# Sliding-window attention and a softplus layer on one core: bias through the matrix engine for the first 512 tokens, and a new order of steps

## Chip, core, metric

The kernel runs on one core of a Trainium2 chip. The metric is the device time of one execution in microseconds; the kernel before takes 218.93 us (median of 3 runs, 218.56 to 219.73). The engines are named as in the profile: PE multiplies matrices (PEld is its load of the stationary operand), DVE works on vectors, ACT evaluates functions, POOL is used here for starting loads, SP for starting stores and transposes by DMA.

## What is computed

Attention over 4 batches of 768 tokens with 8 heads of 64, in which a token sees at most the 96 tokens up to itself and the first 8 tokens of its batch, with a bias that falls with distance; then a two-layer network with a softplus between, on all 3072 tokens.

```python
scores = scale * np.matmul(q, k.transpose(0, 1, 3, 2))
is_global = pos[None, :] < int(n_global)               # 8
is_local = (rel >= 0) & (rel < int(n_local))           # 96
dist = np.where(is_global & ~is_local, float(n_local), np.abs(rel))
bias = -slopes[:, None, None] * dist[None, :, :]       # slopes 2^-1 .. 2^-8
scores = np.where(keep, scores + bias, -1e9)
a = np.exp(scores - max);  a = a / sum;  x = a @ v     # per head, heads side by side: 512 wide
h = x @ w_in                                           # 512 -> 2048
out = softplus(h) @ w_out                              # 2048 -> 512
```

## The kernel before

**Tiling.** The tokens are cut into 24 blocks of 128 (n = 0 to 23, six to a batch) for the attention, and into 12 chunks of 256 (c = 0 to 11, two blocks each) for the network. A block's keys are its own 128 and the block before; the 8 first tokens of the batch are copied over rows of the earlier block that lie outside the window (gk for keys, gv for values). The first block of a batch has its own keys alone.

**The attention of a block**, in halves of four heads: q and k are brought to [feature, token] form, either by transposes on PE through PSUM and copies by DVE (t, blocks 2 to 7; tr_in, to_QT, to_KT), or by DMA transposes that SP starts (d, from block 8 on; dma_qk). sc multiplies keys by queries (16 or 8 matmuls of 64 rows a half, two heads side by side in the array) into the two PSUM banks s_ps; DVE adds the bias table on the way from PSUM to the tile Z in SBUF (add_bias, lines 271 and 273); ACT takes the exponential from Z to Pb (ex, line 295). pv multiplies Pb by the values, with a column of ones for the sum, into x_ps (line 308), and DVE divides (lines 319 and 322). tr_x turns the result to [feature, token] form in XT, on PE for blocks 0 to 5 and by DMA from block 6 on. From block 8 on, sc does both halves at once, the second in two other banks ("tr" and "o2").

**The network.** ffn1 (f) is one of eight steps of a chunk: eight matmuls of 256 columns into one of two banks hT, then on ACT an exponential and a logarithm (lines 358 and 359) into G. ffn2 (o) is one of eight steps: four matmuls of 512 columns into the bank "o" (or "o2"); after four of them DVE copies the bank and SP stores it. Steps are numbered through: f8 is the first of chunk 1. f0, f1 of a chunk need w_in's piece 0, f2, f3 piece 1, and so on; o0 and o4 need w_out's piece 0, o1 and o5 piece 1.

**Loads** are all on POOL's queue and change float32 to bfloat16 on the way: l loads q and k of a block, lv its v, load_w_in and load_w_out a quarter of a matrix. Only block 0's q and k come through SP, as float32 (q_f, k_f), and are cast by DVE (lines 472 and 473). q and k have 4 buffers each in turn, v has 8. In the built program each POOL transfer from the ninth on waits for the landing of the one eight before it. gate (g) holds POOL until a given f step's G is written.

**Order.** A manual schedule: each engine runs its instructions in the order in which the code issues them. `opening()` does the two blocks 0 and 1 with 28 filler matmuls on zeros (warm, 512 columns each; 8 in front, 20 between steps). Bias tables in float32 are made before that, by 24 multiplies on ACT (lines 187 and 191). Then come the steps of the string ORDER, by hand, up to f27, and from there a rule by due times: `steady(n)` for a block (s at 4n - 10.4), f at u + 0.5, o at u + 13.9.

Of the kernel before, what the change touches and what calls it, by code (L numbers as in the profile page):

```python
# [19 lines left out]
def kernel(  # L20
# [11 lines left out]
    nc = tc.nc  # L32
# [50 lines left out]
    q_f = const.tile([P, H, D], F32, name="q_f")  # L83
    k_f = const.tile([P, H, D], F32, name="k_f")
    nc.sync.dma_start(q_f[:], q[0, :, 0:P, :].rearrange("h s d -> s h d"))
    nc.sync.dma_start(k_f[:], k[0, :, 0:P, :].rearrange("h s d -> s h d"))

    def ones(lo, hi):
        for n in range(lo, hi):
# [6 lines left out]
    def load(n, src, dst):  # L96
        b, i = divmod(n, BPB)
        nc.gpsimd.dma_start(  # L98
            dst[n][:, :, 0:D], src[b, :, i * P : (i + 1) * P, :].rearrange("h s d -> s h d")
        )  # L100

    def load_w_in(c):
        nc.gpsimd.dma_start(  # L103
            w_in_c[c][:],
            moe_w_in[:, c * FW : (c + 1) * FW].rearrange("(m p) f -> p m f", p=P),
        )
# [14 lines left out]
    def load_block(n):  # L121
        load_qk(n)
        load_v(n)
# [11 lines left out]


    ident = const.tile([P, P], BF16, name="ident")
    dist_0 = const.tile([P, P], F32, name="dist_0")
    dist_d = const.tile([P, P], F32, name="dist_d")
    dist_p = const.tile([P, P], F32, name="dist_p")  # L140
    bias0 = const.tile([P, 2, 4, P], F32, name="bias0")
    biasA = const.tile([P, 2, 8, P], F32, name="biasA")

    rampf = const.tile([P, P], F32, name="rampf")
    far_a = const.tile([P, P], F32, name="far_a")
# [3 lines left out]
        allow_small_or_imprecise_dtypes=True,  # L149
    )  # L150
    make_identity(nc, ident)
    load(1, q, q_t)
    load(1, k, k_t)
    load(0, v, v_t)
    load(1, v, v_t)
    load_w_in(0)
    load_w_in(1)

    def tables():
        nc.vector.tensor_scalar(  # L160
            far_a[:], rampf[:], float(NL - 1), FAR, op0=ALU.is_gt, op1=ALU.mult
        )
        nc.vector.tensor_scalar(far_b[:], rampf[:], 0.0, FAR, op0=ALU.is_lt, op1=ALU.mult)
        nc.vector.tensor_tensor(far_a[:], far_a[:], far_b[:], ALU.add)
        nc.vector.tensor_tensor(dist_d[:], far_a[:], rampf[:], ALU.add)
        nc.vector.tensor_copy(dist_0[:], dist_d[:])
        nc.vector.tensor_scalar_min(dist_0[0:NG, :], dist_0[0:NG, :], float(NL))
        nc.vector.tensor_scalar(
            far_b[:], rampf[:], -float(P - NL + 1), FAR, op0=ALU.is_gt, op1=ALU.mult
        )  # L170
        nc.vector.scalar_tensor_tensor(dist_p[:], rampf[:], float(P), far_b[:], ALU.add, ALU.add)
        nc.vector.memset(dist_p[0:NG, :], float(NL))

    tables()
    ones(2, RV)

    load_block(2)
    load_block(3)
    load_w_in(2)
    load_w_in(3)  # L180

    def head_of(half, r):
        return 4 * half + 2 * ((r // 2) % 2) + r // 4

    def bias_first(half):
        for r in range(0, 8, 2):
            nc.scalar.mul(bias0[:, half, r // 2, :], dist_0[:], -slopes[head_of(half, r)])

    def bias_rest(half):
        for r in range(8):  # L190
            nc.scalar.mul(
                biasA[:, half, r, :], (dist_p if r % 2 else dist_d)[:], -slopes[head_of(half, r)]
            )

    s_ps = ps.tile([P, 8, P], F32, name="s_ps")
    x_ps = ps.tile([P, 4, D + 1], F32, name="x_ps")
# [7 lines left out]
    def qk_bank():  # L204
        return ps.tile([P, 2, NPAIR, P], BF16, tag="tr", name="tr")

    def tr_in(tr, j, src):
        for m in range(NPAIR):
            nc.tensor.transpose(  # L209
                tr[:, j, m, :], src[:, 2 * m : 2 * m + 2, :].rearrange("p a b -> p (a b)"), ident[:]  # L210
            )

    def to_QT(n, tr):
        QT[n] = work4.tile([P, NPAIR, P], BF16, tag="QT", name="QT")
        nc.vector.tensor_copy(QT[n][:], tr[:, 0, :, :])

    def to_KT(n, tr, copy):
        KT[n] = work4.tile(
            [P, NPAIR, P], BF16, tag="KT0" if n == first_of(n) else "KT", name="KT"
        )  # L220
        copy(KT[n][:], tr[:, 1, :, :])
# [53 lines left out]
    def sc(n, half):  # L275

        qk(n, half, lambda r: s_ps[:, r, :])
        if n < NBT:
            add_bias(n, half)
            return  # L280
        s_lo = ps.tile([P, 4, P], F32, tag="tr", name="s_lo")
        s_hi = ps.tile([P, 4, P], F32, tag="o2", name="s_hi")
        qk(n, 1, lambda r: (s_lo if r < 4 else s_hi)[:, r % 4, :])
        add_bias(n, 0)
        step, bias = (2, bias0) if n == first_of(n) else (1, biasA)
        w = 4 // step
        Z = new_Z(n, 1)
        for i, s_i in enumerate((s_lo, s_hi)):
            regs = slice(i * w, i * w + w)
            nc.vector.tensor_tensor(Z[:, regs, :], s_i[:, 0:4:step, :], bias[:, 1, regs, :], ALU.add)  # L290

    def ex(n, half):
        nreg = 4 if n == first_of(n) else 8
        Pb = work.tile([P, 8, P], BF16, tag="Pb", name="Pb")
        nc.scalar.activation(  # L295
            Pb[:, 0:nreg, :], Zt.pop((n, half))[:, 0:nreg, :], AF.Exp, scale=inv_sqrt
        )
        Pt[n, half] = Pb
# [60 lines left out]
        nc.scalar.activation(G[c][:, 2 * u : 2 * u + 2, :], e_sb[:], AF.Ln, bias=1.0)  # L359

    def o_bank(i):
        return ps.tile([P, DM], F32, tag="o2" if i else "o", name="o")

    def ffn2(c, u):
        if c == NCH - 1 and u >= NWC:
# [41 lines left out]
    def gate(s):  # L407
# [2 lines left out]
        nc.gpsimd.tensor_copy(gate_t[:], G[c][0:1, 2 * u + 1, 0:1])  # L410


    LAG = 13
    KINDS = {
        "t": tr_qk, "d": dma_qk, "gk": gk, "gv": gv, "s": sc, "e": ex, "p": pv, "x": tr_x,
        "l": load_qk, "lv": load_v, "g": gate,
# [2 lines left out]


    ORDER = """
        f0 gv2 gk2 t2 l6 lv6 f1 s2.0 e2.0 f2 t3 l7 lv7 s2.1 e2.1 gk3 f3 p2.0 s3.0 e3.0 f4 p2.1
        gv3 s3.1 e3.1 gk4 f5 x2 p3.0 f6 t4 p3.1 f7 x3 s4.0 f8 f9 e4.0 s4.1 t5 f10 g9 l8 gk5 e4.1
        f11 gv4 o4 p4.0 o0 o1 s5.0 f12 p4.1 o5 o6 e5.0 x4 gv5 s5.1 e5.1 f13 p5.0 o2 t6 o7 p5.1
        s6.0 e6.0 o3 t7 f14 g13 l9 s6.1 d8 p6.0 e6.1 f15 x5 s7.0 o8 o9 p6.1 e7.0 s7.1 gk8 f16
        g15 lv8 d9 p7.0 x6 e7.1 o10 f17 f18 g17 l10 p7.1 f19 s8.0 x7 d10 f20 g19 lv9 e8.0 gv8
        gk9 o11 e8.1 f21 f22 g21 l11 p8.0 s9.0 o12 p8.1 o13 e9.0 gv9 o14 e9.1 f23 p9.0 f24 f25
        p9.1 x8 f26 x9 gk10 gv10 o15 f27
    """

    def steady(n):

        s = 4 * n - 10.4
        return {
            f"d{n}": s - 8.2, f"gv{n}": s - 0.95, f"gk{n}": s - 0.9, f"s{n}.0": s,
            f"e{n}.0": s + 0.7, f"e{n}.1": s + 1.7, f"p{n}.0": s + 1.95, f"p{n}.1": s + 2.95,
            f"x{n}": s + 3.25,
        }

    def run(name):  # L440
        kind = name.rstrip("0123456789.")
        nums = [int(i) for i in name[len(kind):].split(".")]
        if kind in "fo":
            (ffn1 if kind == "f" else ffn2)(*divmod(nums[0], NU))
        else:
            KINDS[kind](*nums)

    warm_ps = ps2.tile([P, DM], F32, tag="hT", name="warm_ps")

    def warm(count):  # L450

        for _ in range(count):
            nc.tensor.matmul(warm_ps[:], warm_in[:, 0:P], warm_in[:])  # L453

    def tr_first_q(n):
        tr = qk_bank()
        tr_in(tr, 0, q_t[n])
        to_QT(n, tr)

    def tr_first_k(n):  # L460
        tr = ps.tile([P, 2, NPAIR, P], BF16, tag="o2", name="tr_k")
        tr_in(tr, 1, k_t[n])
        to_KT(n, tr, nc.vector.tensor_copy if n == 0 else nc.scalar.copy)

    def opening():

        warm(8)
        bias_first(0)
        bias_first(1)
        bias_rest(0)  # L470
        bias_rest(1)
        nc.vector.tensor_copy(q_t[0][:], q_f[:])
        nc.vector.tensor_copy(k_t[0][:], k_f[:])
        tr_first_q(0)
        warm(1)
        tr_first_k(0)
        warm(2)
        sc(0, 0)
        ex(0, 0)
        tr_first_q(1)  # L480
        tr_first_k(1)
        warm(1)
        sc(0, 1)
        ex(0, 1)
        warm(1)
        pv(0, 0)
        sc(1, 0)
        ex(1, 0)
        warm(1)
        pv(0, 1)  # L490
        warm(2)
        sc(1, 1)
        tr_x(0)
        ex(1, 1)
        warm(3)
        pv(1, 0)
        warm(5)
        pv(1, 1)
        warm(3)
        tr_x(1)  # L500
        warm(1)

    opening()
    load_block(4)
    load_block(5)
    for c in range(NWC):
        load_w_out(c)
    first_steps = ORDER.split()
    for name in first_steps:
        run(name)  # L510
    todo = {}
    for n in range(NBT, NB):
        todo.update(steady(n))
    for n in range(RV, NB):
        for name, u in (f"l{n}", 4 * n - 23), (f"lv{n}", 4 * n - 17):
            todo[f"g{u}"] = u + 1.6
            todo[name] = u + 1.7
    for u in range(NU * NCH):
        todo[f"f{u}"] = u + 0.5
        todo[f"o{u}"] = u + LAG + 0.9  # L520
    for name in sorted(todo.keys() - set(first_steps), key=lambda x: (todo[x], x)):
        run(name)


# [33 lines left out]
```

## Time and profile before

| What | us or share |
|---|---|
| median of 3 runs | 218.93 |
| profiled execution, span | 217.8 |
| PE busy | 209.4 (96%) |
| ACT busy | 163.2 (75%) |
| DVE busy | 116.4 (53%) |
| first f matmul starts | 16.11 |
| first f matmul with PE on the chain to the end | 30.55 |
| last store issued | 215.18 |

The costliest groups, as line, engine and operation, output<-input, shape and count, then busy us and mean ns of one, then the idle time in front of them and what ended it:

```profile
L353 PE MATMUL hT<-XT,w_in 128*128 128x256 bf16 x768 | 98.5, 273 | 0.6 <-DVE XT L340 0.3
L373 PE MATMUL o<-w_out,G 128*128 128x512 bf16 x368 | 92.4, 379 | 0.0
L358 ACT ACTIVATE e_sb<-hT 128x512 f32<-128x512 f32 x96 | 56.4, 588 | 23.5 <-PE hT L353 23.2
L295 ACT ACTIVATE Pb<-Z 128x1024 bf16<-128x1024 f32 (+1 forms) x48 | 46.7, 976 | 11.6 <-DVE Z L273 9.4
L273 DVE TENSOR_TENSOR Z<-s_ps,biasA 128x1024 f32<-128x1024 f32 x26 | 31.8, 1222 | 10.7 <-PE s_ps L259 9.2
L453 PE MATMUL warm_ps<-warm_in 128*128 128x512 bf16 x28 | 9.6, 452 | 1.2 <-DVE warm_in L93 1.2
```

A matmul's duration runs to its end, and consecutive matmuls overlap: f matmuls start 0.109 us apart though each lasts 0.273. A PE that is "busy" can therefore still stand between steps, and the distance between starts says what a step costs.

### The profile page before, as it was taken

Reading aid. Unit: us, or ns where it says so; the run is one execution under the profiler, and the core shown is the slowest. Engines: PE = TensorE matmul, PEld = TensorE weight load, DVE = VectorE, ACT = ScalarE, POOL = GpSimd, SP = SyncE. Lnnn points to the kernel's source line nnn. Section 1 sums busy time; section 2 is a strip of 40 time slices with the busy share of each in tenths; the row PEclk is TensorE's granted clock in tenths of the full one; section 3 lists DMA queues with packets and bytes.
Section 4 is the critical chain, followed back from the end, with each engine's and each line's share of the span. In section 5 each row is a group of like instructions: output and inputs, shape, how many; then the busy total and the mean of one; then the engine's idle time right before and its main releaser. Section 6 shows DMA issues by size and latency. Waiting matters only on the chain.

```text
span 217.8 us, 5046 instructions
## 1 busy us (share of the span) xinstructions
PE 209.4 (96%) x2004; PEld 142.0 (65%) x2004; DVE 116.4 (53%) x259; ACT 163.2 (75%) x266; POOL 73.9 (34%) x117
## 2 busy tenths in 40 slices
PE   7788899999999999999999999999999999999993
PEld 2347776666768767666666666666667667666553
DVE  5874965688583454464664664464574573011121
ACT  7737899467999988769779779868978978777200
POOL 8947583331434623524424324333311000000000
PEclk9999999999999999999999999999999999999998
DMA  9999999999999999999999999999992620211112
GB/s 127 162 177 187 172 193 207 164 138 149 109 112 160 150 131 189 128 127 130 143 98 155 140 106 145 145 126 117 154 138 53 98 73 9 66 51 48 48 48 96
DMA packets 110072, 27.06 MB, mean 124 GB/s; under 512 B 102625, under 2 KB 107105, under 8 KB 110049
## 3 DMA queue, kind: packets, MB, share of 16 engines
q0 software_dynamic: 77024, 13.37, 83.2%
q1 hardware_dynamic: 33024, 13.38, 33.5%
q8 instruction: 15, 0.25, 0.5%
q14 instruction: 9, 0.07, 0.1%
HBM read 27.26 MB, written 6.29 MB: 154 GB/s over the span
## 4 chain that ended last, share of the span: by engine, by line
PE 84%; DMA 6%; POOL 4%; ACT 3%; DVE 1%; issue 0%; POOLq 0%; DVEq 0%
PE o L373 37%; PE hT L353 36%; DMA k_t<-in_k_dram 5%; PE x_ps L308 4%; PE s_ps L259 3%; PE s_lo L259 1%; ACT Pb L295 1%; POOL q_t L98 1%; POOL v_t L98 1%; ACT G L359 1%; ACT e_sb L358 1%; PE tr L209 1%; POOL k_t L98 1%; PE o L395 1%; DMA out_dram<-osb 1%; POOL w_in L103 1%
## 5 line engine op out<-in xcount | busy, mean ns | idle before, releaser
L353 PE MATMUL hT<-XT,w_in 128*128 128x256 bf16 x768 | 98.5, 273 | 0.6 <-DVE XT L340 0.3
L373 PE MATMUL o<-w_out,G 128*128 128x512 bf16 x368 | 92.4, 379 | 0.0
L353 PEld LDWEIGHTS <-w_in 128*128 128x128 bf16 x768 | 74.0, 98 | 25.3 <-issue 0.7
L358 ACT ACTIVATE e_sb<-hT 128x512 f32<-128x512 f32 x96 | 56.4, 588 | 23.5 <-PE hT L353 23.2
L359 ACT ACTIVATE G<-e_sb 128x512 bf16<-128x512 f32 x96 | 60.4, 630 | 3.5
L295 ACT ACTIVATE Pb<-Z 128x1024 bf16<-128x1024 f32 (+1 forms) x48 | 46.7, 976 | 11.6 <-DVE Z L273 9.4
L373 PEld LDWEIGHTS <-G 128*128 128x128 bf16 x368 | 32.2, 97 | 27.3
L273 DVE TENSOR_TENSOR Z<-s_ps,biasA 128x1024 f32<-128x1024 f32 x26 | 31.8, 1222 | 10.7 <-PE s_ps L259 9.2
L319 DVE RECIPROCAL rcp<-x_ps 128x4 f32<-128x4 f32 x48 | 8.6, 180 | 49.0 <-PE x_ps L308 49.0
L379 DVE COPY osb<-o 128x512 f32<-128x512 f32 x23 | 15.7, 684 | 25.5 <-PE o L373 25.4
L410 POOL COPY gate_t<-G 1x1 bf16<-1x1 bf16 x32 | 5.7, 177 | 68.7 <-ACT G L359 64.2
L98 POOL DMA_DIRECT2D v_t<-in_v_dram x24 | 21.2, 882 | 6.5 <-PE x_ps L308 2.4
L98 POOL DMA_DIRECT2D q_t<-in_q_dram x23 | 20.4, 887 | 8.4 <-issue 4.5
L98 POOL DMA_DIRECT2D k_t<-in_k_dram x23 | 20.5, 891 | 4.7 <-PE hT L353 1.9
L322 DVE TENSOR_TENSOR xsf<-x_ps,rcp 128x256 bf16<-128x256 f32 x48 | 20.4, 424 | 1.7
L308 PEld LDWEIGHTS <-Pb 128*128 128x128 bf16 x352 | 16.7, 98 | 3.6 <-ACT Pb L295 1.5
L308 PE MATMUL x_ps<-v_t,Pb 128*128 128x65 bf16 x352 | 18.6, 193 | 0.3
L259 PEld LDWEIGHTS <-KT 64*128 64x128 bf16 x352 | 10.3, 94 | 7.5 <-issue 5.5
L259 PE MATMUL s_ps<-QT,KT 64*128 64x128 bf16 x232 | 12.1, 219 | 1.3 <-DVE Z L273 1.0
L453 PE MATMUL warm_ps<-warm_in 128*128 128x512 bf16 x28 | 9.6, 452 | 1.2 <-DVE warm_in L93 1.2
L290 DVE TENSOR_TENSOR Z<-s_hi,biasA 128x512 f32<-128x512 f32 x14 | 9.5, 680 | 0.0
L290 DVE TENSOR_TENSOR Z<-s_lo,biasA 128x512 f32<-128x512 f32 x14 | 9.5, 679 | 0.0
(49 smaller groups left out, 82.5 us busy)
## 6 DMA issues: line engine op xcount, KB each, us to landing
out_dram<-osb SPq DMA_DIRECT2D x23, 256.0 KB, 3.2
v_t<-in_v_dram POOLq DMA_DIRECT2D x24, 128.0 KB, 4.5
q_t<-in_q_dram POOLq DMA_DIRECT2D x23, 128.0 KB, 4.6
k_t<-in_k_dram POOLq DMA_DIRECT2D x23, 128.0 KB, 5.4
w_in<-in_moe_w_in_dram POOLq DMA_DIRECT2D x4, 512.0 KB, 9.8
w_out<-in_moe_w_out_dram POOLq DMA_DIRECT2D x4, 512.0 KB, 10.7
XT<-xsf SPq DMA_TRANSPOSE x18, 4.0
q_f<-in_q_dram SPq DMA_DIRECT2D x1, 256.0 KB, 3.3
```

Source lines behind the costliest of these rows:

```text
L98: nc.gpsimd.dma_start(dst[n][:, :, 0:D], src[b, :, i * P : (i + 1) * P, :].rearrange("h s d -> s h d"))
L259: nc.tensor.matmul(dst(4 * sub + 2 * mm + t), KT[n - t][rows, m, :], QT[n][rows, m, :])
L273: nc.vector.tensor_tensor(Z[:], s_ps[:], biasA[:, half, :, :], ALU.add)
L290: nc.vector.tensor_tensor(Z[:, regs, :], s_i[:, 0:4:step, :], bias[:, 1, regs, :], ALU.add)
L295: nc.scalar.activation(Pb[:, 0:nreg, :], Zt.pop((n, half))[:, 0:nreg, :], AF.Exp, scale=inv_sqrt)
L308: nc.tensor.matmul(x_ps[:, lh, :], Pb[:, r, :], v_t[n - t][:, h, 0 : D + 1], start=(t == 0), stop=(t == 1 or first),)
L322: nc.vector.tensor_tensor(xsf[:, h0 : h0 + 4, :], x_ps[:, :, 0:D], rcp[:, h0 : h0 + 4][:, :, None].to_broadcast([P, 4, D]), ALU.mult,)
L353: nc.tensor.matmul(hT[:, j, :], w_in_c[wc][:, m, fo : fo + P], XT[c][:, m, :], start=(m == 0), stop=(m == KM - 1),)
L358: nc.scalar.activation(e_sb[:], hT[:], AF.Exp)
L359: nc.scalar.activation(G[c][:, 2 * u : 2 * u + 2, :], e_sb[:], AF.Ln, bias=1.0)
L373: nc.tensor.matmul(o[:], G[c][:, 4 * kq + a, ns * P : ns * P + P], w_out_c[kq][:, a, :], start=(kq == 0 and a == 0), stop=(kq == NWC - 1 a ...
L379: nc.vector.tensor_copy(osb[:], O.pop((c, ns))[:])
```

## The change

- Blocks 0 to 3 (the first 512 tokens) get their bias by matmul: the tables are bfloat16, and before the score matmuls of a half, two matmuls with the identity write the bias into the score banks (bias_in); the scores are added to it there (qk_on, start=False). ACT takes the exponential straight from PSUM (ex_on). A second pair of score banks, s2_ps, serves the second half; its pool ends with the fourth block, and the banks "o" and "o2" take its place (ps_o).
- The attention of blocks 0 to 3 stands in front of f0, apart from the last half of block 3. Its value matmuls (pv_in) and divisions (norm) are separate steps, as are transposes (Tq, Tk) and copies (Yq, Yk). x_on puts the transposed x of blocks 0 to 3 through a bank hT.
- Filler: 12 matmuls of 260 columns at the start in place of 28 of 512.
- The second bias table is made by eight multiplies on DVE, of two tables each (BV); only the eight small ones for a batch's first block stay on ACT. k_f is loaded through ACT's queue and cast by ACT.
- POOL's loads are steps of the order (l, lv, i for w_in, u for w_out): ten loads of q, k and v stand ahead of the first quarter of w_in, and the other quarters are spread among the loads of blocks 4 to 7.
- The whole order, to the last step, is written out; the rule by due times is gone.

```diff
-    nc.sync.dma_start(k_f[:], k[0, :, 0:P, :].rearrange("h s d -> s h d"))
+    nc.scalar.dma_start(k_f[:], k[0, :, 0:P, :].rearrange("h s d -> s h d"))
...
-    load(1, q, q_t)
-    load(1, k, k_t)
-    load(0, v, v_t)
-    load(1, v, v_t)
-    load_w_in(0)
-    load_w_in(1)
...
+    def bias_rest(half, mul):
+        for i in range(4):
+            h = 4 * half + 2 * (i % 2) + i // 2
+            mul(biasA[:, half, 2 * i : 2 * i + 2, :], dist[:, OWN : PREV + 1, :], -slopes[h])
...
     ORDER = """
-        f0 gv2 gk2 t2 l6 lv6 f1 s2.0 e2.0 f2 t3 l7 lv7 s2.1 e2.1 gk3 f3 p2.0 s3.0 e3.0 f4 p2.1
...
+        B0:0 B0:1 BV:0 lv0 w12 l1 cq0 b0.0 Tq0 l2 lv1 ck0 Tk0 b0.1 Yq0 Yk0 Tq1 l3 S0.1 S0.0 Tk1
+        E0.0 lv2 lv3 BV:1 P0.0 b1.0 i0 l4 E0.1 Yk1 b1.1 Yq1 i1 N0.0 u0 S1.0 S1.1 P0.1 Tq2 Tk2
+        N0.1 E1.0 l5 gk2 b2.0 P1.0 Yk2 i2 Yq2 S2.0 E1.1 N1.0 P1.1 lv4 N1.1 u1 gv2 b2.1 X0 S2.1
+        E2.0 Tk3 E2.1 P2.0 b3.0 Yk3 Tq3 N2.0 b3.1 P2.1 Yq3 gk3 S3.0 S3.1 l6 E3.0 E3.1 gv3 N2.1
+        X1 X2 lv5 P3.0 N3.0 f0 i3 | l7 P3.1 f1 gk4 N3.1 X3 t4 gv4 u2 f8 s4.0 f9 f10 s4.1 f2 f3
+        o4 t5 e4.0 f11 o0 gk5 u3 lv6 s5.0 e4.1 f12 l8 p4.0 f4 s5.1 e5.0 e5.1 p4.1 f5 o5 gv5 t6
+        l9 o1 p5.0 s6.0 f13 e6.0 x4 l10 p5.1 s6.1 f6 x5 f14 t7 g9 f15 f16 s7.0 f17 o2 lv7 f7
+        e6.1 f18 o6 d8 lv8 e7.0 p6.0 f19 s7.1 o3 o7 p6.1 lv9 e7.1 d9 x6 f20 f21 gk8 s8.0 l11 o8
...
+    def bias_in(n, half):
+
+        dst = in_bank(n, half)
+        for sub in range(2):
+            if n == first_of(n):
+                out_, in_ = dst[:, 4 * sub : 4 * sub + 2, :], bias0[:, half, 2 * sub : 2 * sub + 2, :]
+            else:
+                out_, in_ = dst[:, 4 * sub : 4 * sub + 4, :], biasA[:, half, 4 * sub : 4 * sub + 4, :]
+            nc.tensor.matmul(out_, ident[:], in_, start=True, stop=False)
...
+    def ex_on(n, half):
+        src = in_bank(n, half)
+        Pb = work4.tile([P, 8, P], BF16, tag="Pb", name="Pb")
...
+            nc.scalar.activation(Pb[:], src[:], AF.Exp, scale=inv_sqrt)
+        Pt[n, half] = Pb
...
+    begin, then = ORDER.split("|")
+    with tc.tile_pool(name="ps_s", bufs=1, space=bass.MemoryType.PSUM) as ps_s:
+        second["s"] = ps_s.tile([P, 8, P], F32, name="s2_ps")
+        for name in begin.split():
+            run(name)
+    second["pool"] = ctx.enter_context(
+        tc.tile_pool(name="ps_o", bufs=1, space=bass.MemoryType.PSUM)
+    )
+    for name in then.split():
+        run(name)
```

## The prediction

> **What bounds the kernel now.** I read the page first, then the chain of waits in order of time, then the busy time by stage.
>
> ```profile
> PE 209.4 (96%) x2004; PEld 142.0 (65%) x2004; DVE 116.4 (53%) x259; ACT 163.2 (75%) x266; POOL 73.9 (34%) x117
> PE   7788899999999999999999999999999999999993
> ...
> 10.15 10.44 DMA k_t<-in_k_dram
> 20.64 0.41 PE tr L209 x4
> ...
> 22.99 1.06 ACT Pb L295
> 24.05 0.49 ACT e_sb L358
> 24.57 0.63 ACT G L359
> ...
> 30.55 1.92 PE hT L353 x16
> ...
> 104.82 0.97 PE o L373 x4
> ...
> 112.92 0.97 PE o L373 x4
> ```
>
> TensorE sets the time. From 30.55 us on the chain stays on PE to the end, and a block of 128 tokens takes 112.92 - 104.82 = 8.1 us, of which four f steps (0.87 us each: eight matmuls of 256 columns) and four o steps (0.86 us) are 6.9 us. Only the first 30 us are not PE's: the chain lies on block 3's k, which lands at 10.15 + 10.44 = 20.6 us, and then on ACT.
>
> ```profile
> core 0: us, PE busy (x) PEld busy (x) DVE busy (x) ACT busy (x) POOL busy (x), PEclk, DMA share, GB/s
> 16.11:30.55 14.44, 12.83 (x169) 10.47 (x168) 10.45 (x26) 12.06 (x19) 9.92 (x12) 1.00 1.87 180
> 30.55:72.00 41.45, 41.45 (x439) 29.86 (x440) 26.96 (x59) 34.82 (x55) 16.39 (x26) 1.00 1.49 152
> 72.00:212.60 140.60, 140.60 (x1272) 94.35 (x1270) 66.10 (x136) 106.31 (x164) 34.82 (x59) 1.00 1.01 108
> ```
>
> The first row starts with f0, at 16.11 us. Busy time there counts each matmul to its end, and ends overlap. Counted by the distance between starts (f 0.109 us, transpose 0.056, score 0.041, value 0.030), its 169 matmuls, which are 65 f, 24 and 8 transposes, 40 score and 32 value, are 7.09 + 1.34 + 0.45 + 1.64 + 0.96 = 11.5 us. So PE stood still for about 2.9 us of those 14.4. After that row nothing is left to win but the work itself.
>
> **The sum I make.** The profiled span is 217.8 us = start of f0 + PE's work from there + PE's waits from there + tail (the last copies and stores, which the edit leaves alone). The change moves the first three.
>
> **Start of f0.** Before, two blocks precede it; after, four blocks' scores and the value matmuls up to P3.0. It has two conditions.
> Weights: w_in chunk 0 was POOL's fifth transfer and is now its eleventh, behind ten q, k and v loads.
>
> ```profile
> v_t<-in_v_dram POOLq DMA_DIRECT2D x1, 128.0 KB, 5.1
> w_in<-in_moe_w_in_dram POOLq DMA_DIRECT2D x1, 512.0 KB, 7.2
> w_in<-in_moe_w_in_dram POOLq DMA_DIRECT2D x1, 512.0 KB, 10.6
> w_out<-in_moe_w_out_dram POOLq DMA_DIRECT2D x1, 512.0 KB, 9.9
> w_out<-in_moe_w_out_dram POOLq DMA_DIRECT2D x1, 512.0 KB, 13.3
> ```
>
> These are DMA issues with the us to landing: POOL's fourth load, issued 4.34, landed at 9.4; the weights issued at 5.20, 15.23, 23.54 and 27.78 landed at 12.4, 25.8, 33.4 and 41.1. The last two lie three weights apart: (41.1 - 33.4) / 3 = 2.54 us each. Between 25.8 and 33.4 lie six loads and a weight: (7.6 - 2.54) / 6 = 0.84 us a load. So chunk 0 lands at 9.4 + 6 x 0.84 + 2.54 = 17.0 us.
> Attention: q of block 1 lands at 2.58 + 4.3 = 6.9 us (POOL's second transfer), and in PE's order its transpose precedes block 0's scores. Scores end at 7.4. The exponential follows at once, since the add of 0.69 us (0.22 to 1.2 in other blocks) between them is gone: 7.6 to 8.8 for two of 0.63. Block 1's bias matmul waits for its bank to be read, so the scores end at 9.5 (QT and KT copies of 0.42 each come last) and the exponentials, 1.06 then 0.95, at 11.7. Block 2: bank free 10.7, bias 0.43, copies of QT and KT done 12.0, exponentials 12.6 to 15.0. Block 3: bias in the second bank after 15.0, scores 16.4, first exponential to 17.4, P3.0 0.24, two x transposes 0.45. f0 at about 18.2, so attention ends last, 1.2 us behind the weights. That is +2.1 us.
>
> What no row shows, with both ends: a bias matmul is bounded by 0.109 us (256 columns) and 0.216 (512, the o rows); 4 and 12 of them are 3.0 us of PE, in front of f0, where PE waits anyway; cover gone, about half would be on the path. The exponential from PSUM: e_sb, 512 elements from PSUM, is 0.59 us against 0.63 for an exponential of 512 from SBUF, so between -0.04 and 0 each; I take 0. Eight DVE multiplies of 128x256 lie between a 128x32 copy (0.2) and a 128x512 copy (0.42); 0.2, before DVE has a copy to make. k_f on ACT's queue: SP's issue took 0.57 us, ACT has no other work until the tables at 2.9; the cast on ACT is nearest its KT copy, 0.57 (DVE: 0.79). The eight Z adds removed (two of 0.69, six of 1.22) free 8.7 us of DVE, which was no bound.
>
> **PE's work after f0.** In front of f0 now lie 16 transposes, 32 score and 24 value matmuls of blocks 2 and 3 and 4 transposes of x: 0.90 + 1.31 + 0.72 + 0.22 = 3.15 us less. All f and o steps stay.
>
> **Waits after f0.** The old 2.9 us went to the chain Z add, exponential, value matmul, f on two hT banks; with four blocks done the first f steps have XT 0 and 1 in hand and ACT needs 0.62 + 0.53 = 1.15 us per f, against PE steps mixed with o. So -2.9. New ones: f8 waits for X3's copy, 0.2. Then weights and loads arrive just ahead of use: chunk by chunk from 17.0, w_in 1 at 21.2, w_out 0 23.8, w_in 2 28.0, w_out 1 31.4, w_in 3 36.5, w_out 2 40.7, w_out 3 43.2. PE, counting the new order's steps from 18.2, asks at 23.4, 26.4, 29.8, 33.2, 37.4, 42.8, 47.6: leads of 0.9 to 4.4 us; 0.3 for scatter. The narrow place is d8, the first pair of DMA transposes. Before, 8.9 us of PE steps stood between d8 and s8; now p6.0 f19 s7.1 o3 o7 p6.1 f20 f21 are 5 us.
>
> ```profile
> QT<-q_t SPq DMA_TRANSPOSE x1, 6.2
> KT<-k_t SPq DMA_TRANSPOSE x1, 5.2
> ```
>
> These two (issued at 48.13 and 49.52) landed at 54.3 and 54.7; PE came at 56.95. Now q of block 8 lands at 43.2 + 2 x 0.84 = 44.9, so QT is issued at about 45.5 and KT 1.3 us later, and by these rows KT lands at 52.0; PE is at s8 at 51.1. So 0.9, and 0.2 more for block 11: 1.6 us of new waits in all. Behind the score matmul that waits at s8 stands all of PE, and DVE's adds and ACT's exponentials wait for it; POOL and SP run on. In POOL's queue the q and k loads of blocks 4 to 7 now wait for PE's transposes of blocks 0 to 3 (the last near 15 us), and every transfer from the ninth on for the landing of the one eight before it. Both come some eight transfers, over 7 us, before its turn, so POOL stays ahead of the DMA engines; SP's stores only follow the o steps.
>
> Span: 217.8 + 2.1 - 3.15 - 2.9 + 1.6 = 215.4. The median shown, 218.93, is 1.1 above the span; so 216.5 us.
>
> **A rule against the row.** By the Trainium skill (DMA: Bandwidth & Descriptors, Queues, rings and completion order) each DMA engine goes round robin, packet by packet, among the queues that have work. By that KT of block 8 does not queue behind the loads that POOL has issued, the wait at s8 stays at 0.9 us and the sum at 216.5; the row of 6.2 us, with fewer loads about, agrees only loosely.
>
> **Rivals.**
> *The clock.* The opening loses its 20 filler matmuls of 512 columns between steps; 12 of 260 remain, all at its start.
>
> ```profile
> 4.82:8.23 3.41, 2.37 (x24) 1.18 (x23) 2.16 (x5) 2.96 (x15) 3.41 (x5) 1.00 2.01 133
> 213.03:216.44 3.41, 1.31 (x24) 1.13 (x21) 0.58 (x2) 0.00 (x0) 0.00 (x0) 1.00 0.27 84
> 216.50:217.70 1.20, 0.00 (x0) 0.00 (x0) 0.00 (x0) 0.00 (x0) 0.00 (x0) 0.50 0.00 0
> ```
>
> With 2.37 us busy of 3.4 the full clock was held; after 1.31 of 3.4 the granted clock went to 0.50. Between 4.8 and 8.2 us the new order has some 1.3 us of PE work. If it drops, PE's pieces of the opening chain run at half speed for 3.4 us: some 3 us of pieces, half of them in that stretch, +1.5: 218.0 us. The Trainium skill (TensorE: Matmul & The Clock Gate, Part 1) has the clock fall after an idle window of 3.4 us; PE has none so long here, and by that page the time stays 216.5; the row above is nearer, so I keep the rival.
> *Weights late.* Leads are thin. A transfer service 8% longer puts w_in 3 2.2 us back, past its lead of 0.9; with the chunks behind it +2.2: 218.7. Against: the 2.54 repeated within 0.05 us.
> *Slower: DMA transposes late.* One mechanism: QT and KT by DMA from block 8 on come behind a deeper POOL backlog with less PE work to cover them. If KT of block 8 ends behind the five loads then standing in POOL's queue (k of 8, q and k of 9 and 10: 5 x 0.84 = 4.2 us), and blocks 9 to 11, as tight, wait 0.5 each, that is +5.7: 222.2. For: KT and QT took up to 6.2 us at 48, and DMA is at 9 in every slice to 180 us. Against: in the steady rows at 89 us they land in 3.2 and 4.5. It decides from KT of block 8 landing after 54 us.
> *The edit named first does nothing.* Bias by matmul and exponential from PSUM free DVE, no bound; if the order alone acts, the sum is the same.
>
> **Chances.** Forecast 216.5: 0.55, own range 213.5 to 218. Clock 0.12, weights 0.12, transposes 0.21. About 0.5% (1.1 us) is what can be told from no change. Faster: most of the first and half of the clock, 0.58; same: the rest of those and the weights, 0.20; slower 0.22. The range goes down to 213.5 (f0 at 17.5, no waits) and up to 221 into the transposes.
>
> **What would show it.** f0 at 17.5 to 19; PE idle near nothing from there but at s8 near 51 us; steady blocks still 8.1 us; matmul starts 0.109 apart in f0. It is wrong if PE waits on DMA in more than three places, or f0 starts after 20.

## The result, and the profile after

The changed kernel takes 225.28 us (median of 5 runs, 223.2 to 230.62) against 218.93: ratio 1.0245, 95% interval 1.0215 to 1.0275. It is slower, outside the forecast's range (213.5 to 221.0). The profiled execution is the longest of the five (span 227.7 us; the others are 221.3 to 223.6 us, at mean granted clocks of 1.0 and 0.992), so a second profile of the same kernel stands beside it below (run "again", span 223.6). The times in this document are medians over all executions, while the ratios leave out those that, like this one, lie over 1.5% above the fastest of their group.

First the page of the changed kernel: busy time of the engines, and the tenths of PE and its granted clock in 40 slices of 5.7 us.

```profile
PE 211.7 (93%) x1974; PEld 145.3 (64%) x2004; DVE 107.5 (47%) x259; ACT 159.1 (70%) x250; POOL 74.5 (33%) x120
...
PE   6989999994999993999999999999999999999993
...
PEclk9999999998599998599999999999999999999999
```

Before, PE had no thin slice after the opening. Now there are two, the 10th and the 16th, and with each the clock falls, in it and in the slice behind it. The list of what PE waited for (total, times, longest) says for what:

```profile
PE s_ps L245 <- DMA KT<-k_t: 6.8, 2, 3.4
...
PE hT L339 <- DMA XT<-xsf: 0.3, 1, 0.3
```

Two waits of 3.4 us, for KT of block 8 and of block 12. The stretches around them (length; PE busy, PEld, DVE, ACT, POOL; granted clock; DMA; GB/s):

```profile
19.06:52.80 33.74, 33.46 (x358) 25.36 (x358) 19.68 (x42) 31.04 (x51) 19.39 (x25) 1.00 1.85 177
52.80:56.23 3.43, 0.04 (x1) 0.00 (x0) 0.00 (x0) 1.58 (x3) 0.88 (x1) 0.82 2.39 175
56.23:61.80 5.57, 5.35 (x33) 2.70 (x35) 3.03 (x5) 0.00 (x0) 1.87 (x3) 0.50 2.04 199
61.80:86.30 24.50, 24.03 (x232) 15.48 (x233) 14.76 (x34) 17.29 (x25) 9.59 (x16) 1.00 1.68 128
86.30:89.99 3.69, 0.25 (x3) 0.01 (x2) 0.25 (x2) 0.99 (x2) 1.40 (x4) 0.88 2.01 170
89.99:95.93 5.94, 5.72 (x46) 3.54 (x48) 2.67 (x6) 2.43 (x4) 0.66 (x1) 0.50 1.05 178
95.93:220.00 124.07, 122.86 (x1090) 84.81 (x1108) 52.54 (x115) 95.73 (x150) 23.47 (x47) 1.00 0.71 90
```

From f0 (19.06) to the first wait PE is nearly as full (33.46 of 33.74 us) as it was before from 30.55, so the opening's old standstills are gone as forecast. The loss is in rows two, three, five and six: two waits, and behind each 5.6 and 5.9 us at half clock, in which PE is busy and does half the work (f matmuls start 0.213 us apart there and 0.109 elsewhere, o matmuls 0.427 and 0.216).

Why KT of block 8 is late. SP's queue there (start, duration of the issue), and the us to landing of the transposes issued between 47 and 50 us:

```profile
47.23 2.12 SPq L219 DMA_TRANSPOSE QT<-q_t  x1
49.41 1.25 SPq L220 DMA_TRANSPOSE KT<-k_t  x1
```
```profile
QT<-q_t SPq DMA_TRANSPOSE x1, 7.4
KT<-k_t SPq DMA_TRANSPOSE x1, 6.8
```

QT's issue waits for q of block 8, which landed at 47.1 (forecast 44.9), and lasts 2.1 us; KT follows at 49.4 and lands at 49.41 + 6.8 = 56.2 us. PE was there at 52.8. The time from a transfer's issue to its landing is called its flight below, and the loads that are issued and have not landed the backlog. Why KT of block 12 is late shows the chain of waits (start, us, what):

```profile
80.27 1.28 SPq L219
...
81.64 8.30 DMA KT<-k_t
89.94 0.05 issue
89.99 0.40 PE s_ps L245 x4
```

d12 stands in SP's queue behind x8, d13 and the store of o19, so it is issued at 80.3; KT then takes 8.3 us.

### The profile page after: what moved, and what is told of

It is laid out like the page before. It is cut to its first block, busy times and chain, and to the rows that moved or that the text cites. A ratio compares the mean times of both kernels' runs of the same rounds, so it can differ in the third digit from the quotient of the medians.

```text
span 227.7 us, 4975 instructions
## 1 busy us (share of the span) xinstructions
PE 211.7 (93%) x1974; PEld 145.3 (64%) x2004; DVE 107.5 (47%) x259; ACT 159.1 (70%) x250; POOL 74.5 (33%) x120
## 4 chain that ended last, share of the span: by engine, by line
PE 80%; DMA 14%; DVE 2%; issue 1%; ACT 1%; SPq 1%; DVEq 0%; POOLq 0%; ACTq 0%
PE hT L339 36%; PE o L359 30%; DMA KT<-k_t 4%; PE x_ps L294 4%; DMA QT<-q_t 4%; PE s_ps L245 3%; DMA XT<-xsf 2%; DMA k_f<-in_k_dram 2%; PE s_ps L483 2%; DMA q_t<-in_q_dram 1%; PE s_lo L245 1%; PE x_ps L535 1%; PE tr L195 1%; PE s_ps L495 1%; PE o L381 1%
## 5 line engine op out<-in xcount | busy, mean ns | idle before, releaser
L359 PE MATMUL o<-w_out,G 128*128 128x512 bf16 x340 | 88.9, 388 | 2.0 <-issue 0.8
L339 PEld LDWEIGHTS <-w_in 128*128 128x128 bf16 x768 | 72.6, 98 | 18.8 <-issue 1.2
L359 PEld LDWEIGHTS <-G 128*128 128x128 bf16 x368 | 34.9, 99 | 31.3 <-issue 2.9
L281 ACT ACTIVATE Pb<-Z 128x1024 bf16<-128x1024 f32 (+1 forms) x40 | 38.5, 980 | 7.7 <-DVE Z L257 3.9
L259 DVE TENSOR_TENSOR Z<-s_ps,biasA 128x1024 f32<-128x1024 f32 x20 | 24.5, 1223 | 23.4 <-PE s_ps L245 16.5
L305 DVE RECIPROCAL rcp<-x_ps 128x4 f32<-128x4 f32 x40 | 7.1, 178 | 37.3 <-PE x_ps L294 37.3
L396 POOL COPY gate_t<-G 1x1 bf16<-1x1 bf16 x35 | 6.3, 179 | 56.1 <-ACT G L345 55.2
L294 PEld LDWEIGHTS <-Pb 128*128 128x128 bf16 x296 | 14.7, 100 | 5.3 <-issue 0.6
L308 DVE TENSOR_TENSOR xsf<-x_ps,rcp 128x256 bf16<-128x256 f32 x40 | 17.0, 425 | 1.4
L294 PE MATMUL x_ps<-v_t,Pb 128*128 128x65 bf16 x296 | 16.1, 196 | 0.1
L245 PE MATMUL s_ps<-QT,KT 64*128 64x128 bf16 x176 | 9.6, 228 | 6.8 <-DMA KT<-k_t 6.8
L510 ACT ACTIVATE Pb<-s_ps 128x1024 bf16<-128x1024 f32 x6 | 5.9, 1022 | 4.6 <-PE s_ps L495 4.6
```

The costliest lines, as they stand in the source:

```text
L245: nc.tensor.matmul(dst(4 * sub + 2 * mm + t), KT[n - t][rows, m, :], QT[n][rows, m, :])
L259: nc.vector.tensor_tensor(Z[:], s_ps[:], biasA[:, half, :, :], ALU.add)
L281: nc.scalar.activation(Pb[:, 0:nreg, :], Zt.pop((n, half))[:, 0:nreg, :], AF.Exp, scale=inv_sqrt)
L294: nc.tensor.matmul(x_ps[:, lh, :], Pb[:, r, :], v_t[n - t][:, h, 0 : D + 1], start=(t == 0), stop=(t == 1 or first),)
L308: nc.vector.tensor_tensor(xsf[:, h0 : h0 + 4, :], x_ps[:, :, 0:D], rcp[:, h0 : h0 + 4][:, :, None].to_broadcast([P, 4, D]), ALU.mult,)
L339: nc.tensor.matmul(hT[:, j, :], w_in_c[wc][:, m, fo : fo + P], XT[c][:, m, :], start=(m == 0), stop=(m == KM - 1),)
```

## The experiments

The ratios are to runs of the kernel before beside each group of experiments (medians 219.0, 219.3 and 218.9 us). Edits to ORDER show the part of the line that changed.

**The same kernel again, and the later loads held back.**

```diff
-... d9 x6 f20 f21 gk8 s8.0 l11 o8
+... d9 x6 f20 f21 gk8 s8.0 g21 l11 o8
```

> The changed kernel once more, beside the next three on the same chip. Both theories: 223 to 226 us. What is read from it is the profile: if late DMA transposes and the half clock behind them are the loss, PE waits 3 to 4 us at the scores of block 8 and again at block 12, and the time of each run goes with the time at half clock; if the loss is spread over the schedule, the waits differ from run to run and no two places hold most of it.

> POOL's loads of q and k of block 11 and v of block 13 are held by a gate until f21's G is written; nothing else moves. Theory A (KT of block 8 shares the DMA engines with loads that nobody needs yet): KT lands 2 to 3 us sooner, the wait at block 8 falls from 3.4 to about 1, and with the half clock gone 3 to 6 us come off: 218 to 221. Theory B (KT's latency is SP's own issue and the engines' lag, whatever POOL does): the wait stays over 3 us and the time within 1 us of the changed kernel.

"again": 225.16 us, ratio 1.0204 (1.0115 to 1.0293). Its waits, total 6.0 us, are the same two:

```profile
PE s_ps L245 <- DMA KT<-k_t: 6.0, 2, 3.5
```

"late_loads": 223.51, ratio 1.0123 (1.0058 to 1.0187). KT of block 8 was issued at 49.05 and landed at 55.66, 6.6 us, where it had taken 6.8: the loads that the gate holds, issued about with it and after it, are not what it waits for. Neither theory came true: the wait did not fall to 1 us, and by the ratios the kernel is 0.8% (1.8 us) below "again", though within its interval. Its waits are 3.0 and 2.1 us, but its clock stays full. That is a matter of where the wait falls, shown at the end.

**Block 8 transposed on PE.**

```diff
-... f18 o6 d8 lv8 e7.0 p6.0 f19 s7.1 o3 o7 p6.1 lv9 e7.1 d9 x6 ...
+... f18 o6 lv8 e7.0 p6.0 f19 s7.1 o3 o7 p6.1 lv9 e7.1 t8 d9 x6 ...
```

> Block 8's q and k are transposed by PE and copied by DVE (0.45 us of PE more) instead of the two DMA transposes. Theory A (late KT is the loss at block 8): that wait is gone, and the time falls by 3 to 6 us to 218 to 221. Theory C (the DMA engines are behind as a whole, so the wait only moves on): PE waits as long at block 9 or 10, and the time stays within 1 us.

220.3 us, ratio 1.0069 (1.0046 to 1.0092): by the ratios 1.35% or 3 us below "again", and the intervals lie apart. The wait at block 8 is gone; 1.5 us stand at block 9, whose KT takes 7.1 us, and 1.3 at block 12. So block 8's transposes by DMA are the cause of its wait, and the wait moves on to the next of them in part.

**Block 12's transposes ahead of block 13's.**

```diff
-... f28 x8 d13 lv15 g15 o19 p9.1 gv10 l15 lv11 e10.1 s11.0 d12 e11.1
+... f28 x8 d12 lv15 g15 o19 p9.1 gv10 l15 lv11 e10.1 s11.0 d13 e11.1
```

> The DMA transposes of blocks 12 and 13 change places in SP's queue; nothing else moves. Theory A (block 12's wait is its place behind block 13's and behind a store in SP's queue): KT of block 12 lands about 6 us sooner, that wait of 3.4 us goes with its half clock, 3 to 6 us less: 218 to 221. Theory C (engines behind as a whole): a wait of about 3 us appears at block 13 or elsewhere, time within 1 us.

223.43 us, ratio 1.0119 (1.0058 to 1.0181), above the 218 to 221 of theory A. One wait is left, so the second one came from the order in SP's queue; the first, at block 8, is 3.9 us here, and half clock behind it remains:

```profile
PE s_ps L245 <- DMA KT<-k_t: 3.9, 1, 3.9
```

**Block 8's loads earlier.**

```diff
-... gk5 u3 lv6 s5.0 e4.1 f12 l8 p4.0 ...
+... gk5 lv6 l8 u3 s5.0 e4.1 f12 p4.0 ...
```

> The changed kernel, with only the loads of block 8's q and k moved ahead of the load of the last quarter of w_out (2.55 us of the load stream). Theory A (KT of block 8 is late because its source is late): q8 lands at 44.6 instead of 47.1, KT's transpose is issued at 46.9 instead of 49.4 and lands 6.8 us later, at 53.7; PE waits 0.9 us at block 8 instead of 3.4, no half clock behind it; 225.2 - 2.5 - 2.6 = 220 us, with the wait at block 12 as it was. Theory B (transposes are only served when the stream of loads runs dry): KT lands at 55 to 56 whatever its issue, PE waits 2.5 to 3.5, and the time is 224 to 225.5.

The load of block 6's v moved ahead with them. 223.65 us, ratio 1.0187 (1.0130 to 1.0244). QT was issued at 43.41, KT at 44.76, and KT landed at 52.09, 7.3 us later, with the stream of loads still running; PE did not wait. So theory A holds for block 8: the source's arrival sets the time, the flight is again some 7 us with seven loads in flight, and the transposes do not wait for the stream to end. But the total did not follow (theory A had 220 us), because other transposes took the wait over (timeline of PE; start, us, group, and in brackets the idle time in front):

```profile
60.10 0.40 PE L245 MATMUL s_ps<-QT,KT 64*128 64x128 bf16 x8 [1.55 <-DMA KT<-k_t]
...
84.72 0.40 PE L245 MATMUL s_ps<-QT,KT 64*128 64x128 bf16 x4 [3.77 <-DMA KT<-k_t]
```

Block 9's pair stands in SP's queue behind two stores and is issued at 51.41, no earlier than in "again" (51.31); its KT, issued at 52.68, lands at 60.06; block 12 waits 3.8.

**More filler in the opening, and filler in the wait.**

```diff
-... w12 l1 cq0 b0.0 Tq0 l2 lv1 ck0 Tk0 b0.1 Yq0 Yk0 Tq1 l3 S0.1 ...
+... w12 l1 cq0 b0.0 w4 Tq0 l2 lv1 ck0 w2 Tk0 w3 b0.1 Yq0 Yk0 Tq1 l3 w2 S0.1 ...
```
```diff
-... d9 x6 f20 f21 gk8 s8.0 l11 o8
+... d9 x6 f20 f21 w26 gk8 s8.0 l11 o8
```

> Eleven more filler matmuls of 260 columns between the first steps (4 after b0.0, 2 before Tk0, 3 after it, 2 before S0.1); nothing else moves. Theory: the half clock in the opening is a loss of its own; with the filler full clock comes by 8.5 us in every execution instead of 5 to 12.7, f0 starts at 17.8 to 18.4 instead of up to 19.6, and the time falls by 0.5 to 1 us. Rival: the opening hangs on ACT, DVE and the loads, so f0 stays at 18.2 to 19.6 and the time within 0.5 us of the changed kernel's 225.

> 26 filler matmuls of 260 columns (26 x 0.109 = 2.8 us) in front of block 8's scores, where PE waited 3.4 us; the wait for KT itself stays as it is. If the half clock behind that wait is a loss of its own, it goes and the time falls by 1.7 us (3.4 us at half clock) to 3.4 us (6.8 us at half clock) in the executions that had it: 221.5 to 223.5. If only the idle time counts, the time stays at 224 to 225.5 or rises, since the filler only stands where PE waited.

"fill_open": 223.46, ratio 1.0191 (1.0155 to 1.0227); full clock from 6.4 us, f0 at 18.16, as its theory had them. Filling does not bring f0 further forward: w_in's first quarter had landed at 17.3, but the exponential of block 3 ran to 17.9. An execution of the unchanged kernel with full clock from 5.0 us ("again") has f0 at 18.27 without the filler, and the two ratios (1.0191 and 1.0204) do not tell the times apart. "fill_wait": 222.81, ratio 1.0164 (1.0127 to 1.0202). Here 26 matmuls on zeros stand in the wait, and nothing else is changed:

```profile
53.12 3.04 PE L453 MATMUL x_ps<-warm_in 128*128 128x260 bf16 x26
56.10 0.40 PE L245 MATMUL s_ps<-QT,KT 64*128 64x128 bf16 x8
```

The scores start at 56.1 as with the wait (56.23), but the clock stays full behind them, and the span is 221.2 us where "again" has 223.6. So the half clock is a price of its own, behind the wait. What it is worth is not measured cleanly here: the wait at block 12 is 1.0 us where "again" has 2.5, and f0 is 1.3 us later. By the ratios the gain is 0.8% on the first measurement of the changed kernel, clear of its interval, and 0.4% on "again", within it. The table of sums below prices it.

**The repairs together**, and these with the opening's filler.

> Three edits at once: block 8 transposed by PE, block 11's loads behind f21, block 12's DMA transposes ahead of block 13's. If the waits at blocks 8, 9 and 12 are what the change lost, PE waits under 1 us in all after f0 and the time is 215.5 to 217.5, under the 219 of the kernel before. If another loss lies in the new order, it stays at 218.5 or more.

> The three edits and the eleven fillers of the opening. If the opening's half clock counts, 0.5 to 1 us below the three edits alone: 215 to 216.5. If not, equal within 0.4 us.

"all3" (block 8 on PE, later loads held back, block 12 first): 219.83 us, ratio 1.0022 (0.9998 to 1.0046). "all4": 219.97, 1.0046 (1.0020 to 1.0071). What PE waits for in "all3" after f0 (18.43):

```profile
PE hT L339 <- DMA XT<-xsf: 0.7, 1, 0.7
...
PE s_ps L245 <- DMA KT<-k_t: 0.5, 1, 0.5
```

With most of the waits gone the change is level with the kernel before, no faster. The 215.5 to 217.5 us expected of it were missed, and the opening's filler is worth nothing that can be told.

"all3" and "pe_t8" also show what makes a transpose late. Up to block 9 they differ in one thing: "all3" holds the loads from block 11 on back until f21. Block 9's pair is issued at 51.3 and 53.3 us in "pe_t8", with five loads in flight at KT's issue, and at 51.5 and 52.9 in "all3", with one. Us to landing, first "pe_t8", then "all3":

```profile
QT<-q_t SPq DMA_TRANSPOSE x1, 8.5
KT<-k_t SPq DMA_TRANSPOSE x1, 7.1
```
```profile
QT<-q_t SPq DMA_TRANSPOSE x1, 3.6
KT<-k_t SPq DMA_TRANSPOSE x1, 2.7
```

Holding the loads back takes 4 to 5 us off. It could not help block 8's pair: of the seven loads in flight when the changed kernel issues its KT, six stand ahead of the gate.

**f0 ahead of block 3's attention.**

```diff
-... lv2 lv3 BV:1 P0.0 b1.0 i0 l4 ...
+... lv2 BV:1 P0.0 b1.0 i0 lv3 l4 ...
-... Yq3 gk3 S3.0 S3.1 l6 E3.0 E3.1 gv3 N2.1 X1 X2 lv5 P3.0 N3.0 f0 i3 |
+... Yq3 gk3 X1 S3.0 S3.1 l6 E3.0 E3.1 gv3 N2.1 f0 X2 lv5 P3.0 N3.0 i3 |
-... o15 f24 lv12 f25 lv10 g23 o16 o17 p8.1 f26 gv9 g15 s10.0 d11 p9.0 e10.0 f27 o18 ...
+... o15 p8.1 f24 lv12 f25 lv10 g23 o16 o17 f26 gv9 g15 f27 s10.0 d11 p9.0 e10.0 o18 ...
```

> The three repairs, and four moves: the first weights' load ahead of block 3's values, XT of block 1 ahead of block 3's scores, f0 in front of block 2's transposes and block 3's attention, f27 ahead of the scores of block 10 and the second half of block 8's attention ahead of f24. Theory A (what is left over the kernel before is the later f0 and two small waits): w_in0 lands one load of 0.86 us earlier, f0 starts at 17.5 instead of 18.4, the waits of 0.8 at f24 and 0.7 at block 10 shrink to 0.3 together: 219.8 - 0.9 - 1.2 = 217.7 us, ratio 0.993 to the kernel before. Theory B (the opening is bound by the attention chain of four blocks, not by the place of f0): the work that f0 now stands ahead of waits as long behind it, and the time stays at 219.8.

220.36 us, ratio 1.0050 (1.0019 to 1.0081). f0 started at 17.43, as intended, and nothing was won: PE waits 0.8 us for the division of block 3 right behind it, and 1.2 for XT and KT. Theory B holds.

**The bias by VectorE instead.** In "all3", the 16 bias matmuls are left out, and behind each half's scores stands

```diff
+        Z = new_Z(n, half)
...
+            nc.vector.tensor_tensor(Z[:], dst[:], biasA[:, half, :, :], ALU.add)
```

with the exponential from Z.

> The kernel with the three repairs (block 8 transposed on PE, late loads gated, block 12's transposes ahead of block 13's), but with the bias of the first four blocks added by VectorE (one add from the score bank into a tile in SBUF behind each half's scores, exponential from there), and without the 16 bias matmuls. Theory A (bias by matmul is what lets four blocks stand in front of the first layer): VectorE has about 8 us of work between 8.0 us and f0 there; two adds of 0.7 us and six of 1.23 us put 8.8 us more on it, so f0 would start at about 8 + 8 + 8.8 = 25 us instead of 18.4, and the time would be 219.8 + 6 = 226 us. Theory B (the rival of the forecast: the bias edit does nothing, since VectorE has room): f0 within 1 us of 18.4 and 219 to 221 us.

228.46 us, ratio 1.0455 (1.0411 to 1.0499); f0 at 26.98 instead of 18.43. The stretch from 8 us to f0, first "z_add", then "all3" (columns as above):

```profile
8.00:26.98 18.98, 10.91 (x137) 8.47 (x134) 15.62 (x37) 7.49 (x8) 14.00 (x17) 1.00 1.74 176
```
```profile
8.00:18.43 10.43, 9.37 (x141) 6.35 (x141) 7.85 (x25) 6.53 (x8) 9.12 (x11) 1.00 1.97 165
```

DVE has 15.6 us of work in front of f0 in place of 7.9, and its adds are the largest part of the chain of waits to f0. PE, with more holes, is at full clock only from 29.45 us (the column's 1.00 for "z_add" is not a measurement, as its record of the clock begins there; transposes start 0.107 us apart before it and 0.056 behind it). That is part of the 8.6 us: an estimate is 2 to 3 us, half of the some 5 us that PE's pieces take on that chain. The rest is near the 6 us that theory A had for the adds. The bias by matmul is what allows four blocks in front of f0 at this price.

**The filler of the kernel before.** Its 20 warm matmuls between steps left out.

> The kernel before without the 20 filler matmuls between the steps of its opening (the 8 at the start stay). Theory A (they hold the clock): the clock is full 3.4 to 6.8 us later than 4.8, the opening's matmuls take twice as long until then, f0 starts at 16.8 to 17.5 instead of 16.1 and the time is 219.8 to 220.6. Theory B (they only fill idle time): f0 at 15.9 to 16.2 and 218.9 to 219.2 us.

221.33 us, ratio 1.0106 (1.0072 to 1.0140). f0 is not moved (16.20), but the clock falls at 9.42, after a stretch in which PE was 2.0 us busy, and is full again only at 19.66:

```profile
6.01:9.42 3.41, 2.02 (x32) 1.23 (x29) 2.52 (x7) 3.26 (x12) 3.41 (x5) 1.00 1.74 148
9.42:16.20 6.78, 3.38 (x39) 2.30 (x38) 5.03 (x12) 2.36 (x3) 4.06 (x5) 0.50 1.66 178
16.20:19.66 3.46, 3.46 (x21) 2.71 (x21) 0.92 (x4) 1.23 (x2) 3.08 (x4) 0.50 2.13 170
```

So the old fillers were worth 2.4 us. Theory A was right that they hold the clock and wrong in the rest: the clock was full from 6.01, was lost again for 10.24 us, f0 did not move and the time is above its 220.6.

## Why the prediction was wrong

The forecast's sum, with what each run measured put into it: 217.8 + (f0 - 16.11) - 3.15 - 2.9 + PE's waits for QT, KT and XT after f0 + half of the time at half clock in which PE worked + 0.45 for eight transposes where block 8 is on PE.

| Kernel | f0 | waits | half clock | sum | span |
|---|---|---|---|---|---|
| changed kernel | 19.06 | 7.1 | 5.5 | 227.3 | 227.7 |
| again | 18.27 | 6.0 | 3.1 | 223.0 | 223.6 |
| late_loads | 18.79 | 5.6 | 0 | 220.0 | 220.6 |
| d12_first | 19.57 | 4.1 | 1.6 | 220.9 | 221.2 |
| l8_early | 18.36 | 5.3 | 1.4 | 220.7 | 221.0 |
| pe_t8 | 18.25 | 2.9 | 0 | 217.2 | 217.6 |
| all3 | 18.43 | 1.2 | 0 | 215.7 | 216.1 |
| z_add | 26.98 | 1.4 | 1.2 | 225.7 | 226.0 |

The sum's form held within 0.6 us in these eight. Four others come out 1.0 to 2.3 us short: "fill_open" 221.1 against 222.1, "all4" 215.7 against 217.9, "fill_wait" 219.2 against 221.2 (its 3.0 us of filler counted as wait) and "best1" 214.7 against 217.0. In the first three the stretch from PE's last matmul to the end was 4.3, 4.9 and 5.2 us, where the other runs have 3.4 to 3.6; in "best1" part of the work that -3.15 stands for lies behind f0 again.

"again" took 225.32 us, 8.8 above the forecast: 4.4 us are waits, 3.1 half clock, 0.1 the start of f0, 0.7 the step from span to time, and 0.5 no term names. Point by point:

- *Work moved ahead of f0, -3.15, and old waits, -2.9:* right as a pair, since the sums close; each alone was not measured.
- *Start of f0, 18.2:* near. It was 18.2 to 19.6 in the runs with this order of attention and a bias by matmul. Attention ends last in the first profile, but w_in's first quarter landed at 18.1 there, not 17.0, and in "again" f0 waits 0.6 us for it, to 18.2. The slowest of the 16 DMA engines landed 0.7 us behind the first for the earliest loads of the first profile, 2.1 for this one and 3.1 from 30 us on. Where the clock is full only from 10 to 12.7 us, f0 is at 18.8 to 19.6.
- *New waits, "So 0.9, and 0.2 more for block 11: 1.6 us of new waits in all":* this is the step that failed. They were 6.0 to 7.1 us. At block 8 the 0.9 was 3.0 to 3.9. In the first profile KT was issued 2.6 us later than worked out (q landed 2.2 us late, and QT's issue took 2.1 us), its flight was 6.8 us where the row of 5.2 was taken, and PE came 1.7 us later than forecast: 0.9 + 2.6 + 1.6 - 1.7 = 3.4. The trace of before held longer flights, at 70 to 75 us:

```profile
QT<-q_t SPq DMA_TRANSPOSE x2, 7.4
KT<-k_t SPq DMA_TRANSPOSE x1, 7.4
```

  The price came from the pair that stood in the same place in the old order. Two loads were in flight when its KT was issued, and seven in the new order. The second wait is at block 12, not 11: d12's place in SP's queue, behind x8, d13 and a store, wasn't priced.
- *What follows a wait:* the sum had nothing for it. PE works at half clock for up to 5.9 us behind a long wait, and half of that time is lost: 3.1 us in "again", 5.5 in the first profile.
- *From span to median, +1.1:* 217.8 is the span of one execution of the kernel before and 218.93 the median time of several. Where time and span of one execution are known, they differ by 1.7 to 1.8 us for the kernel before and by 2.0 in the changed kernel's median execution (225.28 and 223.3). So 0.9 us of the miss lies here.
- *Its own signs of being wrong,* DMA waits in more than three places or f0 after 20, did not show: there were three places and f0 was at 19.06. They asked how many waits there are, and the loss was in how long two of them are.
- *The rule of the Trainium skill* (DMA: Bandwidth & Descriptors, Queues, rings and completion order: round robin among the queues with work) was taken to leave the wait at 0.9. Shares of the engines' time are not the flight of one transfer: each KT that PE waited over 1 us for, in all runs, took 5.9 to 8.5 us, against 2.4 for the KT that before issued at 54.06, with one load in flight. The measurement decides against the use made of it. That holding back later loads changed block 8's flight by 0.2 us, and that KT landed at 52.09 in "l8_early" in the middle of the stream, is no evidence against round robin itself. By what mechanism the backlog holds a transpose up stays open.
- *Rival "DMA transposes late":* this is what happened, with its sign (KT of block 8 landed at 56.2 and 55.5, after its 54). Its +5.7 is near the waits (6.0 to 7.1) in part by luck: it had 4.2 at block 8 and 0.5 at each of the next three, and the waits were some 3 us each at blocks 8 and 12. It lacked the clock, and so fell short: 222.2 against 225.3.
- *Rival "the clock":* wrong in its place, since the opening does reach f0 by 18.2 to 19.6 without the fillers between steps; right in its mechanism, which acts behind the waits. "before_nofill" shows that it would have cost the old opening 2.4 us.
- *Rival "weights late":* no. PE waited on weights 0.6 us at most, in front of f0.
- *Rival "the bias edit does nothing":* no; 8.6 us (z_add), part of them the clock's.

Why the repaired kernel is level and not 2 us faster, as the profile of "all3" (216.1 against 217.8) and its sum would have it, stays open. The two profiles come from opposite ends: 216.1 is the shortest of ten spans (to 218.9, median 217.7), and 217.8 is above the median of the kernel before beside it (217.5 of 216.9 to 218.3). The ten do not go by the clock: at a mean of 1.0 they are 216.1 to 218.4 us long, at 0.985 to 0.992 216.5 to 218.9. One possible part is a longer end. The fourth store from the end, of 256 KB, takes 2.0 us in twelve of the fourteen traces and took 4.1 and 4.5 in two, with a copy waiting for its buffer (the chain of waits, "all4" and "fill_wait"):

```profile
210.20 4.09 DMA out_dram<-osb
```
```profile
213.23 4.51 DMA out_dram<-osb
```

Whether that happened in the other executions is not shown, as they have no trace.

## What to carry to other kernels

Price a moved transfer by its flight under the backlog that it will meet in the new order, and follow every queue it goes through (its source's load, the issuing queue, the DMA engines); a row from the same place in the old order is no measure of it. A wait on PE of some 3 us can cost more than its length, because the clock can fall behind it: either cover it with work, even idle matmuls, or count half of the next 3.4 or 6.8 us. And where one late transfer is put right, look for the next one in the same queue before counting the gain.

## What the runs showed of the hardware

The flight of a DMA transpose goes with the number of loads in flight when it is issued. Over the 219 KT transposes of all fourteen traces its median is 2.9 us with none or one of POOL's loads in flight, 4.7 with two or three, 6.5 with four, and 7.4 (6.2 to 8.5) with five or more. The scatter is wide below five: one took 7.4 with two.

The clock goes by stretches of 3.41 us that run free of the program: each spell at half clock, but for those at the very end, was 3.41, 6.83 or 10.24 us, and the full clock came anywhere from 5.0 to 12.7 us in the same opening. Cut into these stretches, the rows of PE explain why one wait is punished and another, as long, is not. First the changed kernel (wait at block 8, then at block 12), then "late_loads" (PE's own columns: length, busy, granted clock, DMA, GB/s):

```profile
51.56:54.97 3.41, 1.28 (x12) 1.00 2.61 129
...
85.69:89.10 3.41, 0.85 (x4) 1.00 2.01 180
```
```profile
50.95:54.37 3.42, 1.79 (x18) 1.00 1.84 105
54.37:57.78 3.41, 2.05 (x29) 1.00 1.56 259
81.67:85.08 3.41, 1.83 (x19) 1.00 1.80 117
```

After 1.28 and 0.85 us of work in a stretch the clock fell; in "late_loads" the wait of 3.0 us lay across the border of two, with 1.79 and 2.05 us in them, and the clock held. The other runs agree: 0.71, 1.06, 1.10, 0.22 and 0.00 us were followed by half clock, 1.85 and 1.90 not. The opening does not fit that line (2.02 us there, of short matmuls, were followed by half clock in "before_nofill"), so busy time alone is not the measure. The Trainium skill (TensorE: Matmul & The Clock Gate, Part 1) has the free-running window of 3.4 us and the fall after an idle one; the window agrees, but here a window with 1.28 us of work was enough.
